# A fused two-layer MLP: the opening loads re-ordered over two queues, with the first transposes gathered ahead of the first matmuls

## The chip, the cores and the metric

The kernel runs on one core of one Trainium2 chip. The metric is the device time of one execution in microseconds (us). The kernel before has a median of 291.05 us in 8 runs (290.72 to 291.46).

## What is computed

```python
B, S, D, F = 1, 2048, 576, 4608          # all tensors bf16
h = einsum("bsd,df->bsf", x, w1) + b1
r = where(h > 0, h, 0)
h = r * r                                 # squared relu
out = einsum("bsf,fd->bsd", h, w2) + b2
```

## The kernel before, in words

The 2048 rows of x are worked on in four blocks of 512 (`SB`). For each block, phase A computes the hidden layer transposed, 36 tiles of 128 hidden features by 512 rows, and phases T and B multiply it with w2. Phase T (`phase_t`) makes the last 128 output columns, phase B (`phase_b`) the other 448. Blocks 0 and 1 go through phase A, then through T and B; then blocks 2 and 3 do the same.

The inner dimension of the first product is 576, four and a half times 128. The first four of the 36 hidden tiles (`a_full`) are computed with four matmuls over 128 inner rows each, and the odd 64 rows with two matmuls that sit side by side in the upper and the lower half of the array (`pair`, L203 and L205). The other 32 hidden tiles (`a_rows`, L188 and L190) split all of the inner dimension into nine pieces of 64 rows, again two matmuls side by side. Because of these halves the transposed x, `xTw`, holds several of its 128-row windows twice, shifted by 64 partitions; the second copies are made by `dup_windows` (L119, L120).

ScalarE takes each hidden tile out of PSUM with bias and relu (L176), VectorE squares it (L177).

The transposed x of blocks 1 to 3 comes from DMA transposes (L126, L127). Block 0 is different, since TensorE would have to wait for these. Its four tiles of 128 rows (`x_sb`) are loaded plainly, transposed on TensorE against an identity (L149) into PSUM banks `tb`, and copied to `xTw` by VectorE (L156, L159) and ScalarE (L158). In the branch `k_outer` of `a_full` the matmuls of the first four hidden tiles are cut into pieces of 256 rows of x (`part(h, k)`, L227, 4 matmuls each) and written out by hand between the transposes: ten transposes (x tiles 0 and 1), part (0,0), five transposes (x tile 2), parts (0,1) and (0,2), five transposes (x tile 3), the parts (0,3) and (1,0), the transpose of the bias rows (`make_b1T`, L166), the rest of the parts, and the two pairs. Until x arrives, TensorE runs seven matmuls on constants (`WARM`, L61 to L63) whose result is not used.

Loads, in their order on each queue:
- SyncE's queue (SP): x tile 0, w1n chunk 0, w1n chunk 1, x tile 3, w1n chunks 2 and 3 (w1n is w1 for the first four hidden tiles, one chunk for each 128 inner rows), two loads of `w_h` (w1 for the other hidden tiles), two loads of `w1n8` (w1's last 64 rows for the first four hidden tiles, in runs of 256 bytes), and the rest of w_h, with the DMA transposes of block 1 between; then the bias b2, w2 in four chunks (`w_sb`), and block 2.
- ScalarE's queue: x tiles 1 and 2, ahead of its activation-table load and a one-element activation (`warm`, L104).
- GpSimd's queue (POOL): the bias b1 as 36 rows of 256 bytes (L98), and 128 single elements of b2 (L100). GpSimd also makes the identity, zeroes the bias rows and converts b2's elements (L102).

`keep` holds the order as written on each engine. `tc.tile_pool` deals out the buffers: PSUM's eight banks are two pools of four, `ps_h` (tag ph) and `ps_o` (tag po).

Of the kernel before, what the change touches and what calls it, by code (L numbers as in the profile page):

```python
# [17 lines left out]
def kernel(  # L18
# [40 lines left out]
    wps = ps_o.tile([P, 512], FP32, name="wps", tag="po")  # L59
    ones = nc.const_aps.tensor(1.0, [P, 512], BF16)  # L60
    WARM = [512] * 6 + [128]  # L61
# [5 lines left out]
    w1n8 = wpool.tile([P, G // 2, P], BF16, name="w1n8")  # L67
# [6 lines left out]
    def load_w1n(eng, k):  # L74
        keep(eng.dma_start(out=w1n[:, k, :], in_=w1[k * P:(k + 1) * P, 0:GW]))  # L75

    def load_w1n8(eng, h):
        src = w1[NK * P:D, 0:GW].rearrange("p (i h f) -> p i h f", h=2, f=P)
        keep(eng.dma_start(out=w1n8[h * H:(h + 1) * H, :, :], in_=src[:, :, h, :]))
# [4 lines left out]

    load_x(nc.sync, 0)
    load_x(nc.scalar, 1)
    load_w1n(nc.sync, 0)
    load_x(nc.scalar, 2)
    load_w1n(nc.sync, 1)
    load_x(nc.sync, 3)  # L90
    for k in range(2, NK):
        load_w1n(nc.sync, k)
# [3 lines left out]
    b1_rows = const.tile([P, P], BF16, name="b1_rows")  # L96
    nc.gpsimd.memset(b1_rows[:], 0.0)
    nc.gpsimd.dma_start(out=b1_rows[0:NFT, :], in_=b1.rearrange("(ft p) -> ft p", p=P))  # L98
    b2_col = const.tile([P, 1], BF16, name="b2_col")
    nc.gpsimd.dma_start(out=b2_col[:], in_=b2[DM:D].rearrange("(d o) -> d o", o=1))  # L100
    b2T = const.tile([P, 1], FP32, name="b2T")
    nc.gpsimd.tensor_copy(out=b2T[:], in_=b2_col[:])  # L102
    warm = const.tile([P, 1], FP32, name="warm")
    keep(nc.scalar.activation(out=warm[:], in_=nc.const_aps.tensor(0.0, [P, 1], FP32), func=ACT.Relu))  # L104

# [25 lines left out]
    W2CH = 9  # L131
# [9 lines left out]
    tb_po = [ps_o.tile([P, 2, HS], BF16, name="tb", tag="po") for _ in range(2)]  # L141
    tb_ph = [ps_h.tile([P, 2, HS], BF16, name="tb", tag="ph") for _ in range(4)]
    half_banks = [tb_ph, None]

    def x_transpose(j, k):
        h, q = divmod(j, 2)
        qc = slice(q * P, (q + 1) * P)
        bank, slot, c0 = (half_banks[h][k], 0, k * P) if k < NK else (half_banks[h][2], 1, D - P)
        keep(nc.tensor.transpose(bank[:, slot, qc], xs[:, j, c0:c0 + P], ident[:]))  # L149

    def x_copies(h):
        hc = slice(h * HS, (h + 1) * HS)
        for k in range(NK):
            src = half_banks[h][k][:, 0, :]
            if k % 2 == 0:
                keep(nc.vector.tensor_copy(out=xT0[:, O + k, hc], in_=src))  # L156
            else:
                keep(nc.scalar.copy(out=xT0[:, O + k, hc], in_=src))  # L158
        keep(nc.vector.tensor_copy(out=xT0[:, E3, hc], in_=half_banks[h][2][:, 1, :]))  # L159


    b1T = const.tile([P, NFT], FP32, name="b1T")

    def make_b1T():
        b1T_ps = ps_o.tile([P, P], BF16, name="b1T_ps", tag="po")
        keep(nc.tensor.transpose(b1T_ps[:], b1_rows[:], ident[:]))  # L166
        keep(nc.vector.tensor_copy(out=b1T[:], in_=b1T_ps[:, 0:NFT]))
# [27 lines left out]
    def a_full(sb, order):  # L195
        xT = xT_blk[sb]
        banks = []
        for g in range(G):
            pool, tag = (ps_o, "po") if g < 2 else (ps_h, "ph")
            banks.append(pool.tile([P, SB], FP32, name="pn", tag=tag))  # L200

        def pair(i, start, stop):
            keep(nc.tensor.matmul(banks[2 * i][:], lhsT=w1n8[0:H, i, :], rhs=xT[0:H, SPC, :],  # L203
                             start=start, stop=stop, skip_group_check=order == "k_outer"))
            keep(nc.tensor.matmul(banks[2 * i + 1][:], lhsT=w1n8[H:P, i, :], rhs=xT[H:P, E3, :],  # L205
                             start=start, stop=stop, skip_group_check=order == "k_outer"))
# [12 lines left out]
        else:  # L219
            if order == "k_outer":  # L220
                tb_new = [ps_h.tile([P, 2, HS], BF16, name="tb", tag="ph") for _ in range(2)]
                half_banks[1] = tb_new + tb_po

# [7 lines left out]
                for j in range(2):  # L231
                    for k in range(NK):
                        x_transpose(j, k)
                for j in range(2):
                    x_transpose(j, NK)
                x_copies(0)
                part(0, 0)
                for k in range(NK + 1):
                    x_transpose(2, k)
                part(0, 1)  # L240
                part(0, 2)
                for k in range(NK + 1):
                    x_transpose(3, k)
                x_copies(1)
                dup_windows(0)
                part(0, 3)
                part(1, 0)
                make_b1T()
                for k in range(1, NK):
                    part(1, k)  # L250
            else:
# [42 lines left out]
    for (j0, j1) in [(0, 1), (1, 2), (2, 4), (4, 6), (6, 8), (8, 10), (10, 12)]:  # L294
        load_w1(nc.sync, 0, j0, j1)
        load_w1(nc.sync, 1, j0, j1)
        if j0 == 0:
            load_w1n8(nc.sync, 0)
            load_w1n8(nc.sync, 1)
    load_xT(1)  # L300
    for (j0, j1) in [(12, 14), (14, 16)]:
        load_w1(nc.sync, 0, j0, j1)
        load_w1(nc.sync, 1, j0, j1)
    keep(nc.sync.dma_start(out=b2_bc[:], in_=b2.partition_broadcast(P)))
    for c in (0, 2, 1, 3):
# [54 lines left out]
```

## Time and profile before

| | us |
|---|---|
| median of 8 runs | 291.05 |
| lowest and highest | 290.72, 291.46 |
| the profiled execution itself | 290.99 |
| its span, first to last instruction | 289.2 |
| TensorE busy in the span | 284.8 (98%) |
| ScalarE busy | 96.6 (33%) |
| VectorE busy | 78.5 (27%) |
| GpSimd busy | 2.2 (1%) |

All durations come from that one profiled execution. A timeline row gives the start, the time from its first start to its last end, the engine, the line, what is written and read, and how often; consecutive equal instructions are merged. The end of a matmul is modelled and overlaps the next one, so the pace of a run of matmuls is read from start to start. In the timeline "SPq" and "ACTq" are the two engines' DMA issues; the transfer itself comes later.

### The profile page before, as it was taken

What the parts mean: (1) busy time and instruction counts of PE and PEld (TensorE: products, weight loads), DVE (VectorE), ACT (ScalarE), POOL (GpSimd) and SP (SyncE); (2) the same over time, 40 slices, a digit from 0 to 9 for tenths busy, and PEclk for the clock granted to TensorE, in tenths of its full rate; (3) what the DMA queues carried; (4) which work ended last, traced back from release to release, by engine and by line L of the source; (5) the groups of instructions that cost most, each with busy time, mean ns of one, the idle gap of its engine ahead of it and who ended that gap; (6) DMA issues with size and microseconds to landing.
All of it is one profiled execution on the core that took longest, in us unless ns stands there. A gap on an engine that the chain in (4) does not pass through costs nothing.

```text
span 289.2 us, 4693 instructions
## 1 busy us (share of the span) xinstructions
PE 284.8 (98%) x2027; PEld 138.8 (48%) x2032; DVE 78.5 (27%) x176; ACT 96.6 (33%) x154; POOL 2.2 (1%) x10
## 2 busy tenths in 40 slices
PE   8999999999999999999999999999999999999996
PEld 4544444444444555555544444444444455555555
DVE  1644544444500200000025444444440001100001
ACT  3666666666500000000027666666670000000000
POOL 3000000000000000000000000000000000000000
PEclk9999999999999999999999999999999999999999
DMA  6999999700001100000000000000000110000000
GB/s 192 219 232 173 261 387 271 121 0 2 0 18 28 44 16 18 16 16 18 16 16 2 1 2 0 2 0 2 0 2 0 36 39 16 16 16 20 32 16 18
DMA packets 31605, 16.52 MB, mean 57 GB/s; under 512 B 15700, under 2 KB 31584, under 8 KB 31584
## 3 DMA queue, kind: packets, MB, share of 16 engines
q1 hardware_dynamic: 31232, 15.91, 22.7%
q8 instruction: 16, 0.26, 0.4%
q10 hardware_dynamic: 288, 0.30, 0.3%
q14 instruction: 5, 0.04, 0.0%
q0 software_dynamic: 64, 0.01, 0.0%
HBM read 11.36 MB, written 2.36 MB: 47 GB/s over the span
## 4 chain that ended last, share of the span: by engine, by line
PE 97%; DMA 1%; SPq 1%; issue 0%; DVE 0%
PE po L289 38%; PE ph L188 24%; PE ph L190 19%; PE pt L270 11%; PE pn L209 4%; DMA w1n<-in_w_dram 1%; PE pn L227 1%; PE pn L203 1%; SPq L75 0%; SPq L72 0%; PE pn L205 0%; DVE o_sb L291 0%; PE tb L149 0%; PE b1T_ps L166 0%
## 5 line engine op out<-in xcount | busy, mean ns | idle before, releaser
L190 PE MATMUL ph<-xTw,w_h 64*128 64x512 bf16 x576 | 124.8, 376 | 0.0
L188 PE MATMUL ph<-xTw,w_h 64*128 64x512 bf16 x576 | 124.7, 376 | 0.0
L289 PE MATMUL po<-w_sb,hT 128*128 128x448 bf16 (+2 forms) x612 | 109.4, 341 | 0.0
L176 ACT ACTIVATE r<-ph,b1T 128x512 bf16<-128x512 f32 x128 | 81.0, 684 | 41.8 <-PE ph L190 22.7
L289 PEld LDWEIGHTS <-hT 128*128 128x128 bf16 x612 | 58.5, 98 | 51.0
L177 DVE TENSOR_TENSOR hT<-r 128x512 bf16<-128x512 bf16 x144 | 61.2, 425 | 76.2 <-ACT r L176 75.6
L188 PEld LDWEIGHTS <-w_h 64*128 64x128 bf16 x576 | 54.1, 94 | 38.5
L190 PEld LDWEIGHTS <-w_h 64*128 64x128 bf16 x576 | 54.1, 94 | 30.0 <-DMA w_h<-in_w_dram 0.4
L291 DVE TENSOR_TENSOR o_sb<-po,b_bc 128x448 bf16<-128x448 f32 (+2 forms) x17 | 10.2, 597 | 125.8 <-PE po L289 125.8
L270 PE MATMUL pt<-hT,w_sb 128*128 128x512 bf16 x142 | 31.3, 379 | 0.1
L176 ACT ACTIVATE r<-pn,b1T 128x512 bf16<-128x512 f32 x16 | 10.3, 687 | 61.2 <-PE pn L205 59.6
L270 PEld LDWEIGHTS <-w_sb 128*128 128x128 bf16 x144 | 14.1, 98 | 17.0
L273 ACT ACTIVATE oT<-pt,b2T 128x512 bf16<-128x512 f32 x4 | 2.7, 687 | 28.3 <-PE pt L270 28.3
L209 PE MATMUL pn<-xTw,w1n 128*128 128x512 bf16 x45 | 10.4, 379 | 0.4 <-issue 0.3
L209 PEld LDWEIGHTS <-w1n 128*128 128x128 bf16 x48 | 4.5, 98 | 6.0 <-issue 0.8
L227 PE MATMUL pn<-xTw,w1n 128*128 128x256 bf16 x32 | 4.2, 273 | 0.5 <-DMA w1n<-in_w_dram 0.4
L63 PE MATMUL wps<-const-bfloat16-1.0 128*128 128x512 bf16 (+1 forms) x7 | 2.8, 579 | 0.8 <-PEq L344 0.8
L227 PEld LDWEIGHTS <-w1n 128*128 128x128 bf16 x32 | 2.9, 98 | 1.1 <-DMA w1n<-in_w_dram 0.6
L119 DVE COPY xTw<-xTw 64x2048 bf16<-64x2048 bf16 x4 | 2.8, 690 | 0.2
L120 DVE COPY xTw<-xTw 64x2048 bf16<-64x2048 bf16 x4 | 2.8, 688 | 0.1
L156 DVE COPY xTw<-tb 128x256 bf16<-128x256 bf16 x4 | 1.1, 291 | 6.0 <-PE tb L149 6.0
L203 PE MATMUL pn<-xTw,w1n 64*128 64x512 bf16 x8 | 2.4, 379 | 0.0
(23 smaller groups left out, 13.7 us busy)
## 6 DMA issues: line engine op xcount, KB each, us to landing
w_sb<-in_w_dram SPq DMA_DIRECT2D x4, 1296.0 KB, 12.7
w_h<-in_w_dram SPq DMA_DIRECT2D x14, 288.0 KB, 6.2
out_dram<-o_sb SPq DMA_DIRECT2D x15, 112.0 KB, 1.7
w_h<-in_w_dram SPq DMA_DIRECT2D x4, 144.0 KB, 3.6
w1n<-in_w_dram SPq DMA_DIRECT2D x4, 128.0 KB, 3.2
out_dram<-ot SPq DMA_DIRECT2D x4, 128.0 KB, 2.0
x_sb<-in_x_dram ACTq DMA_DIRECT2D x2, 144.0 KB, 3.1
x_sb<-in_x_dram SPq DMA_DIRECT2D x2, 144.0 KB, 3.2
```

Of the source, the lines that this page charges most:

```text
L63: keep(nc.tensor.matmul(wps[:, 0:n], lhsT=ones[:, 0:P], rhs=ones[:, 0:n], start=True, stop=True))
L119: keep(nc.vector.tensor_copy(out=xT[0:H, SPC:SPC + 4, :], in_=xT[H:P, E3:E3 + 4, :]))
L176: keep(nc.scalar.activation(out=r[:], in_=bank[:], func=ACT.Relu, bias=b1T[:, ft:ft + 1], scale=1.0))
L177: keep(nc.vector.tensor_tensor(out=hTs[sb][:, ft, :], in0=r[:], in1=r[:], op=ALU.mult))
L188: keep(nc.tensor.matmul(bx[:], lhsT=w1_h[0:H, LO_C[i], jc], rhs=xT[0:H, LO_W[i], :], start=(i == 0), stop=(i == NC - 1)))
L190: keep(nc.tensor.matmul(by[:], lhsT=w1_h[H:P, UP_C[i], jc], rhs=xT[H:P, UP_W[i], :], start=(i == 0), stop=(i == NC - 1)))
L203: keep(nc.tensor.matmul(banks[2 * i][:], lhsT=w1n8[0:H, i, :], rhs=xT[0:H, SPC, :], start=start, stop=stop, skip_group_check=order == "k_o ...
L209: keep(nc.tensor.matmul(banks[g][:], lhsT=w1n[:, k, g * P:(g + 1) * P], rhs=xT[:, O + k, :], start=start, stop=stop))
L227: keep(nc.tensor.matmul(banks[g][:, hc], lhsT=w1n[:, k, g * P:(g + 1) * P], rhs=xT[:, O + k, hc], start=(h == 0 and k == 0), stop=False, s ...
L270: keep(nc.tensor.matmul(pt[:], lhsT=w2_sb[:, ft, DM:D], rhs=hT[:, ft, :], start=(i == 0), stop=(i == NFT - 1)))
L289: keep(nc.tensor.matmul(po[:, 0:d1 - d0], lhsT=hT[:, ft, jj * P:(jj + 1) * P], rhs=w2_sb[:, ft, d0:d1], start=(i == 0), stop=(i == NFT - 1)))
L291: keep(nc.vector.tensor_tensor(out=o_sb[:, d0:d1], in0=po[:, 0:d1 - d0], in1=b2_bc[:, d0:d1], op=ALU.add))
```

## The change

- **x on SP.** All four x tiles go first on SyncE's queue, in order.
- **w1n and b1 on ScalarE's queue.** It issues b1 (its rows zeroed by VectorE now, not GpSimd) and then the four w1n chunks, all of it ahead of the activation-table load.
- **GpSimd loads nothing.** The 128 elements of b2 are loaded on SyncE's queue, behind the last of w_h; GpSimd still converts them.
- **w1n8** is loaded ahead of w_h, as 64 rows of 1024 bytes, twice (all four tiles' columns in both halves of the partitions). w2 comes in two chunks, not four.
- **Transposes.** All 16 full transposes of the four x tiles stand ahead of part (0,0). The odd 64 columns of x are gathered by GpSimd into `xs8`, two x tiles side by side, and cost two transposes in place of four (`transpose_tails`), behind part (0,1).
- **Copies.** Two of eight PSUM copies are ScalarE's, in place of four of eight. The window copies of block 0 are one on ScalarE (1536 elements), and on VectorE four small ones out of PSUM, one of 2048 and one of 512 elements, in place of the two of 2048 elements.
- **Banks.** All transposes use `ps_h`, and the four accumulators of `a_full(0)` use `ps_o`.
- **Warm-up.** Five matmuls of 512 columns and one of 256, in place of six of 512 and one of 128.

```diff
-    wps = ps_o.tile([P, 512], FP32, name="wps", tag="po")
+    wps = ps_h.tile([P, 512], FP32, name="wps", tag="ph")
-    WARM = [512] * 6 + [128]
+    WARM = [512] * 5 + [256]
...
-    w1n8 = wpool.tile([P, G // 2, P], BF16, name="w1n8")
+    w1n8 = wpool.tile([P, GW], BF16, name="w1n8")
...
-        src = w1[NK * P:D, 0:GW].rearrange("p (i h f) -> p i h f", h=2, f=P)
-        keep(eng.dma_start(out=w1n8[h * H:(h + 1) * H, :, :], in_=src[:, :, h, :]))
+        keep(eng.dma_start(out=w1n8[h * H:(h + 1) * H, :], in_=w1[NK * P:D, 0:GW]))
...
+    b1_rows = const.tile([P, P], BF16, name="b1_rows")
+    nc.vector.memset(b1_rows[:], 0.0)
     load_x(nc.sync, 0)
-    load_x(nc.scalar, 1)
-    load_w1n(nc.sync, 0)
-    load_x(nc.scalar, 2)
-    load_w1n(nc.sync, 1)
-    load_x(nc.sync, 3)
-    for k in range(2, NK):
-        load_w1n(nc.sync, k)
+    keep(nc.scalar.dma_start(out=b1_rows[0:NFT, :], in_=b1.rearrange("(ft p) -> ft p", p=P)))
+    for rt in range(1, RT):
+        load_x(nc.sync, rt)
+        load_w1n(nc.scalar, rt - 1, rt)
+    load_w1n(nc.scalar, NK - 1, NK)
...
-    b1_rows = const.tile([P, P], BF16, name="b1_rows")
-    nc.gpsimd.memset(b1_rows[:], 0.0)
-    nc.gpsimd.dma_start(out=b1_rows[0:NFT, :], in_=b1.rearrange("(ft p) -> ft p", p=P))
-    b2_col = const.tile([P, 1], BF16, name="b2_col")
-    nc.gpsimd.dma_start(out=b2_col[:], in_=b2[DM:D].rearrange("(d o) -> d o", o=1))
-    b2T = const.tile([P, 1], FP32, name="b2T")
-    nc.gpsimd.tensor_copy(out=b2T[:], in_=b2_col[:])
...
+    for h in range(2):
+        load_w1n8(nc.sync, h)
+    xs8 = const.tile([P, RT, H], BF16, name="xs8")
+    for h in range(2):
+        keep(nc.gpsimd.tensor_copy(out=xs8[:, 2 * h:2 * h + 2, :], in_=xs[:, 2 * h:2 * h + 2, NK * P:D]))
...
-    W2CH = 9
+    W2CH = 18
...
+    tb = [[ps_h.tile([P, 4, HS], BF16, name="tb", tag="ph") for _ in range(2)] for _ in range(2)]
+
+    def x_transpose(j):
         h, q = divmod(j, 2)
         hc = slice(h * HS, (h + 1) * HS)
+        for bank in range(2):
+            for k in range(2 * bank, 2 * bank + 2):
+                keep(nc.tensor.transpose(tb[h][bank][:, k % 2, q * P:(q + 1) * P], xs[:, j, k * P:(k + 1) * P], ident[:]))
+            for k in range(2 * bank, 2 * bank + 2) if q == 1 else ():
+                copy = nc.scalar.copy if h == 1 and bank == 1 else nc.vector.tensor_copy
+                keep(copy(out=xT0[:, O + k, hc], in_=tb[h][bank][:, k % 2, :]))
...
+    def dup_windows_first():
+        keep(nc.scalar.copy(out=xT0[0:H, E:E + 3, :], in_=xT0[H:P, O:O + 3, :]))
+
+    def transpose_tails():
+        tl = ps_h.tile([P, 2, P], BF16, name="tl", tag="ph")
+        for h in range(2):
+            keep(nc.tensor.transpose(tl[:, h, :], xs8[:, 2 * h:2 * h + 2, :], ident[:]))
+        x8 = xT0.rearrange("p c (h q t) -> p c h q t", h=2, q=2)
+        for q in range(2):
+            keep(nc.vector.tensor_copy(out=x8[H:P, E3, :, q, :], in_=tl[q * H:(q + 1) * H, 0:2, :]))
+        for q in range(2):
+            keep(nc.vector.tensor_copy(out=x8[0:H, SPC, :, q, :], in_=tl[q * H:(q + 1) * H, 0:2, :]))
+        keep(nc.vector.tensor_copy(out=xT0[H:P, SPC:SPC + 4, :], in_=xT0[0:H, O:O + 4, :]))
+        keep(nc.vector.tensor_copy(out=xT0[0:H, E3, :], in_=xT0[H:P, O + 3, :]))
...
-            pool, tag = (ps_o, "po") if g < 2 else (ps_h, "ph")
+            pool, tag = (ps_o, "po") if g < 2 or order == "k_outer" else (ps_h, "ph")
...
-                for j in range(2):
-                    for k in range(NK):
-                        x_transpose(j, k)
-                for j in range(2):
-                    x_transpose(j, NK)
-                x_copies(0)
+                for j in range(RT):
+                    x_transpose(j)
+                dup_windows_first()
                 part(0, 0)
-                for k in range(NK + 1):
-                    x_transpose(2, k)
                 part(0, 1)
+                transpose_tails()
                 part(0, 2)
-                for k in range(NK + 1):
-                    x_transpose(3, k)
-                x_copies(1)
-                dup_windows(0)
                 part(0, 3)
-                part(1, 0)
-                make_b1T()
-                for k in range(1, NK):
+                for k in range(NK):
                     part(1, k)
+                    if k == 1:
+                        make_b1T()
...
-        if j0 == 0:
-            load_w1n8(nc.sync, 0)
-            load_w1n8(nc.sync, 1)
...
+    b2_col = const.tile([P, 1], BF16, name="b2_col")
+    keep(nc.sync.dma_start(out=b2_col[:], in_=b2[DM:D].rearrange("(d o) -> d o", o=1)))
+    b2T = const.tile([P, 1], FP32, name="b2T")
+    keep(nc.gpsimd.tensor_copy(out=b2T[:], in_=b2_col[:]))
     keep(nc.sync.dma_start(out=b2_bc[:], in_=b2.partition_broadcast(P)))
-    for c in (0, 2, 1, 3):
+    for c in range(2):
         load_w2(c)
```

## The prediction

> **What bounds the kernel now.** I read four views in this order. First the page and its chain of work that ended last: TensorE is busy all along.
>
> ```profile
> PE 284.8 (98%) x2027; PEld 138.8 (48%) x2032; DVE 78.5 (27%) x176; ACT 96.6 (33%) x154; POOL 2.2 (1%) x10
> PE   8999999999999999999999999999999999999996
> PE 97%; DMA 1%; SPq 1%; issue 0%; DVE 0%
> ```
>
> The only slice below nine tenths, other than the last, is the first, which is where the change lies. So the whole question is when TensorE starts a_rows(0), its first matmul at L188; what follows is the same work in the same order, at TensorE's pace. Second, TensorE's timeline of the opening.
>
> ```profile
> 0.78 2.82 PE L63 MATMUL wps<-const-bfloat16-1.0 128*128 128x512 bf16 x7 [0.78 <-PEq L344]
> 3.61 0.73 PE L149 MATMUL tb<-ident,x_sb 128*128 128x128 bf16 x10
> 4.44 0.60 PE L227 MATMUL pn<-xTw,w1n 128*128 128x256 bf16 x4
> 4.87 0.45 PE L149 MATMUL tb<-ident,x_sb 128*128 128x128 bf16 x5
> 5.16 0.60 PE L227 MATMUL pn<-xTw,w1n 128*128 128x256 bf16 x4
> 6.11 0.61 PE L227 MATMUL pn<-xTw,w1n 128*128 128x256 bf16 x4 [0.35 <-DMA w1n<-in_w_dram]
> ...
> 7.76 1.47 PE L227 MATMUL pn<-xTw,w1n 128*128 128x256 bf16 x12
> 9.17 0.39 PE L203 MATMUL pn<-xTw,w1n 64*128 64x512 bf16 x1
> ...
> 9.40 0.38 PE L203 MATMUL pn<-xTw,w1n 64*128 64x512 bf16 x1
> ...
> 9.61 0.38 PE L188 MATMUL ph<-xTw,w_h 64*128 64x512 bf16 x1
> ```
>
> x tile 0 releases TensorE at 3.61, a_rows(0) begins at 9.61: 6.00 us. Paces, start to start: a transpose (0.73-0.22)/9 = 0.057 us, a 256-column matmul (1.47-0.27)/11 = 0.109, a pair 0.22. The work is 20 transposes (1.13), 32 part matmuls (3.49), the bias transpose (0.06), two pairs (0.44): 5.12. The other 0.88 is idle: about 0.27 before 4.44 (the first PSUM copy), 0.52 before 6.11 (w1n chunk 2, which lands at 6.06), 0.10 before 9.17 (full to half array).
>
> Third, the transfers: the tile view of x_sb, and the stretches of the opening (the last two columns are the DMA share and GB/s).
>
> ```profile
> DMA to landing us min/median/max: 2.8/3.1/3.6
> ```
> ```profile
> 1.75:2.50 0.75, 0.75 (x4) 0.21 (x2) 0.00 (x0) 0.75 (x1) 0.75 (x2) 1.00 0.74 114
> 2.50:4.25 1.75, 1.74 (x14) 0.84 (x13) 0.15 (x1) 0.75 (x3) 0.17 (x1) 1.00 1.05 368
> 4.25:5.00 0.75, 0.65 (x9) 0.52 (x8) 0.61 (x3) 0.55 (x2) 0.00 (x0) 1.00 0.98 223
> ```
>
> x tile 3, issued at 2.13, is the 3.6: it lands at 5.73. The rate drops from 368 to 223 GB/s where the GpSimd queue's small packets run (3.7 to 5.2 us). Fourth, a_rows(0) has one late weight:
>
> ```profile
> 17.38 0.38 PE L188 MATMUL ph<-xTw,w_h 64*128 64x512 bf16 x1
> 17.67 0.39 PE L190 MATMUL ph<-xTw,w_h 64*128 64x512 bf16 x1
> ```
>
> 0.29 where the pace is 0.22: 0.07 us lost to a w_h load that lands at 17.62.
>
> **What the Trainium skill says.** "DMA: Bandwidth & Descriptors", Issuing engines are not separate DMA queues: queues of different engines share the same DMA engines, and a second queue saves issue time only. The trace agrees: two queues together move 368 GB/s in the opening, SP alone moves up to 392 later. "TensorE: Matmul & The Clock Gate", What's actually happening: the array runs at half clock until it was busy through a window of about 3.4 us, and the windows run freely. The trace agrees: warm-up matmuls start 0.43 apart, twice the later 0.216, and its clock record has full clock from 3.57 for 286.72 us, which is 84 windows of 3.413. "VectorE: DVE Perf Modes", the TRN2 errata: a ScalarE copy between SBUF tiles costs (224 + elements)/1.2 ns; no row here shows one.
>
> **The change, part by part.**
>
> *TensorE.* All 16 full transposes now stand ahead of part (0,0), so it waits for x tile 3. Call its landing T3. Behind it remain: wake-up 0.05 (6.06 to 6.11 above), tile 3's transposes 4 x 0.057 = 0.23, parts 3.49, two tail transposes 0.11, bias 0.06, array change 0.10, pairs 0.44: 4.48. The stalls of 0.27 and 0.52 go, and two transposes (0.11). Break-even with 9.61 is T3 = 5.13, which is 0.60 earlier than now.
>
> *T3.* SP issues four x tiles at its pace of today (0.73, 1.20, 1.66, 2.13), so tile 3 is issued no earlier than now; only what lies ahead of it changes. ScalarE's issues of 0.41 to 0.47 bring b1 and w1n 0 to 2 (402 KB) from about 0.95, behind VectorE's memset. At 2.50 some 86 KB (114 GB/s x 0.75) of the 590 KB of x have moved; from there both queues take half of 368. After 402/184 = 2.18 us, at 4.68, ScalarE's three chunks are through, and the last 102 KB take 0.28 at full rate: 4.96. From last packet to landing it was 0.36 (5.37 to 5.73): T3 = 5.32, take 5.30. This assumes that the dip to 223 goes with the GpSimd loads; if it stays, (368-223) x 0.75 = 109 KB, or 0.30 more. Bounds: 4.8 (issue 2.13 plus the shortest landing in the trace, 2.7) to 5.8 (dip stays, and w1n chunk 3 shares the rate). So a_rows(0) starts at 5.30 + 4.48 = 9.78: **+0.17** (from -0.33 to +0.67).
>
> *New waits.* Transfers of the two hardware queues use eight semaphores in turn, and an issue waits for the landing eight places ahead: today w_h's first issue waits for x tile 1 until 3.74. In the new order w1n 3 waits for x tile 0 (about 3.5), and behind it on ScalarE stand table load (1.28), warm (0.20) and copies: ready near 5.5, needed near 5.8, nothing lost. w1n 3 lands near 5.8, needed by part (0,3) near 7. b1's wait for the memset (0.20 for this size on GpSimd) has w1n behind it; that is in the 0.95. On SP, w1n8 waits for tile 0 and b1 (3.5), then 1; w_h follows near 4.5, 0.8 later than now, and lands near 8.5, needed at 9.8. w_h's wide loads then start near 7.35, where they start at 7.87, because w1n8's issues (2 x 0.65) are no longer between: the load that lands at 17.62 comes some 0.5 earlier and the stall at 17.4 goes: **-0.07**.
>
> *VectorE, ScalarE, GpSimd.* After T3 VectorE has two PSUM copies (0.57), then from tail transposes at T3+1.4 four small ones (4 x 0.29, half the partitions of a row at 0.29), 0.69 (L120's row), 0.25 for 512 elements (between 0.20 and 0.69), bias 0.20: done at T3+3.8; the pairs come at T3+4.0 and need only the small ones, T3+2.6. ScalarE: two copies (0.75) to T3+1.2, then 1536 elements, an estimate from the skill's price of (224+1536)/1.2 = 1.47: T3+2.7, its readers at T3+5.3. GpSimd's gathers are 128 x 128, bounded by the affine select of that size (0.28) and 1.0; cover to T3+1.1. All at nothing, but the cover is thin on VectorE: every us more there than 0.2 to 1.4 would go straight to the path.
>
> *Elsewhere.* b2's column on SP delays b2, w2 and the x transposes by an issue (0.4 to 0.9); w2 has its last issue at 36.3, lands within 13.6, and is first read at 76.1. Nobody waits behind GpSimd's conversion until 84.1. The w2 chunks are as many bytes. PSUM slots: each reuse is of a bank that was emptied over 1 us before. All nothing.
>
> Sum: 290.99 + 0.17 - 0.07 = 291.09; the median lies 0.06 above the profiled execution: **291.15**.
>
> **The rivals.** The measurement can tell about 0.2%, 0.58 us, from no change; 290.47 and 291.63 are the limits.
>
> *x comes sooner (0.13).* Without the dip and with tile 0 alone at the front, T3 could be 4.8: 9.28, so -0.33 - 0.07: 290.65. For it: SP's packets are x alone. Against: half the rate goes to w1n. It passes 290.47 only with T3 below 4.6, about half of this case.
>
> *The clock rises late (0.16), the other side.* The warm-up ends near 0.78 + 0.38 + 4 x 0.43 + 0.21 = 3.09, where it ended at 3.6, and until T3 TensorE has 12 transposes only. In the window 0.15 to 3.57 it was busy 2.79 of 3.41 us, 82%; now 2.3 to 2.4, 69%. It decides if 69% doesn't open the gate: the next window ends at 6.98, and half pace from 5.3 to there costs 1.68/2 = 0.84: 292.0. Still another window: 2.5, 293.6. Up to T3 a late gate is free.
>
> *Local copies bind (0.06).* VectorE's chain or GpSimd's gather is over 1.4 late against T3+4.0: about +0.7, 291.9.
>
> *The dip stays (0.05).* T3 = 5.8: +0.50, 291.6.
>
> **How the numbers follow.** The forecast case has 0.60. Faster by over 0.2%: half of the first rival, 0.07. Slower: 0.15 of the clock, 0.05 of the copies, 0.01 of the dip: 0.21. Within: 0.72. Range: 290.5 (T3 4.7 and the runs' spread) to 292.0 (clock one window late), leaving about 0.17 out.
>
> **What would show it.** Right: x tile 3 lands near 5.3, part (0,0) starts by 5.6, no gap among the 32 parts, L188 starts at 9.8, no 0.29 step near 17.5, no rate dip at 4.25 to 5. Wrong: T3 below 4.8 or above 5.6; transposes or parts at 0.11 or 0.21 pace behind T3 (clock); an idle gap before the tails or L203 (copies); any stall after 12 us that is new.

## The result, and the profile after

The changed kernel is slower: a median of 293.4 us (291.76 to 294.66, 11 runs) beside 291.01 for the kernel before (290.58 to 291.61, 31 runs). The ratio, which is one of means, is 1.0075, 95% interval 1.0062 to 1.0089, or 1.8 to 2.6 us. The spread grew too, from 1.0 to 2.9 us. The profiled execution took 293.40 us, its span is 291.5; that of before took 290.99. So the two profiles differ by 2.41 us, as the medians do (2.39), and the working below uses the profiles.

The page of the kernel after, busy time, the row of slices, and the chain that ended last:

```profile
PE 285.6 (98%) x2024; PEld 139.8 (48%) x2029; DVE 79.3 (27%) x181; ACT 97.4 (33%) x153; POOL 1.5 (1%) x9
PE   6999999999999999999999999999999999999996
PE 97%; DMA 2%; SPq 0%; issue 0%; DVE 0%
```

TensorE still sets the end and is as full as before in all slices but the first, which fell from 8 tenths to 6, and the chain now has 2% of DMA. The loss is in the opening. TensorE's timeline of it (the transposes are L146 now, the parts L228, the tails L159, the pairs L207 and L209, a_rows L192 and L194):

```profile
0.77 2.51 PE L63 MATMUL wps<-const-bfloat16-1.0 128*128 128x512 bf16 x6 [0.77 <-PEq L338]
3.07 1.06 PE L146 MATMUL tb<-ident,x_sb 128*128 128x128 bf16 x8
5.67 0.61 PE L146 MATMUL tb<-ident,x_sb 128*128 128x128 bf16 x4 [1.54 <-DMA x_sb<-in_x_dram]
6.78 0.61 PE L146 MATMUL tb<-ident,x_sb 128*128 128x128 bf16 x4 [0.51 <-DMA x_sb<-in_x_dram]
7.18 1.91 PE L228 MATMUL pn<-xTw,w1n 128*128 128x256 bf16 x8
8.89 0.36 PE L159 MATMUL tl<-ident,xs 128*128 128x128 bf16 x2
9.08 1.91 PE L228 MATMUL pn<-xTw,w1n 128*128 128x256 bf16 x16
...
10.88 1.04 PE L228 MATMUL pn<-xTw,w1n 128*128 128x256 bf16 x8
11.85 0.39 PE L207 MATMUL pn<-xTw,w1n 64*128 64x512 bf16 x1
...
12.29 0.38 PE L192 MATMUL ph<-xTw,w_h 64*128 64x512 bf16 x1
```

Two things are to be seen. TensorE waits 1.54 us for x tile 2 and 0.51 for x tile 3. And behind tile 3 it runs at half pace: the first eight of the parts' matmuls take 1.91 us, as long as the sixteen that begin at 9.08. The trace's clock record has full clock from 9.04; before it was 3.57. Below, the moment from which the record shows full clock is called the opening of the clock gate. a_rows(0) begins at 12.29, where it began at 9.61: 2.68 later. The tile view of x_sb in the kernel after, and then its opening in two stretches, up to 2.50 and on to 6.37, which is 0.36 before x tile 3 lands (last column GB/s):

```profile
DMA to landing us min/median/max: 2.2/3.1/4.6
```
```profile
0.00:2.50 2.50, 1.73 (x5) 0.65 (x6) 0.11 (x1) 0.00 (x0) 0.70 (x6) 1.00 0.26 70
2.50:6.37 3.87, 2.23 (x15) 1.30 (x13) 0.88 (x4) 1.49 (x2) 0.29 (x1) 1.00 0.90 263
```

Tile 3, issued at 2.12, is the 4.6: it lands at 6.73 (before 5.73). The stretch moved 263 GB/s. PEclk is 1.00 in both: the column doesn't show the half pace, the matmuls' starts and the clock record do.

Later on, time comes back. The place of the late w_h load, now at 20 us, shows no step, and at the switch from a_rows(1) to the next `a_full`, at 72 us in the kernel before and 74 us in the kernel after, the two half-array streams stand differently. First before, then after:

```profile
71.85 0.38 PE L190 MATMUL ph<-xTw,w_h 64*128 64x512 bf16 x1
71.85 0.38 PE L203 MATMUL pn<-xTw,w1n 64*128 64x512 bf16 x1
72.07 0.38 PE L205 MATMUL pn<-xTw,w1n 64*128 64x512 bf16 x1
72.07 0.38 PE L203 MATMUL pn<-xTw,w1n 64*128 64x512 bf16 x1
72.28 0.38 PE L205 MATMUL pn<-xTw,w1n 64*128 64x512 bf16 x1
```
```profile
74.24 0.38 PE L192 MATMUL ph<-xTw,w_h 64*128 64x512 bf16 x1
74.24 0.38 PE L194 MATMUL ph<-xTw,w_h 64*128 64x512 bf16 x1
74.45 0.38 PE L207 MATMUL pn<-xTw,w1n 64*128 64x512 bf16 x1
74.46 0.38 PE L209 MATMUL pn<-xTw,w1n 64*128 64x512 bf16 x1
```

Before, the lower half's last L190 runs beside the upper half's L203, and a lone L205 is left at 72.28 with nothing beside it. The stall at 17.4 had put the halves one matmul out of step, and they stayed so. After, they are in step and the slot of 0.21 us is not spent. With the 0.08 of the stall itself that is -0.29. Experiment 4 shows that this need not be the change's doing. The sum: +2.68 - 0.29 = +2.39, and the last matmul moved from 286.27 to 288.66, by +2.39.

### The profile page after: what moved, and what is told of

Read it like the earlier page. It is cut to its first block, busy times and chain, and to the rows that moved or that the text cites. A ratio compares the mean times of both kernels' runs of the same rounds, so it can differ in the third digit from the quotient of the medians.

```text
span 291.5 us, 4693 instructions
## 1 busy us (share of the span) xinstructions
PE 285.6 (98%) x2024; PEld 139.8 (48%) x2029; DVE 79.3 (27%) x181; ACT 97.4 (33%) x153; POOL 1.5 (1%) x9
## 4 chain that ended last, share of the span: by engine, by line
PE 97%; DMA 2%; SPq 0%; issue 0%; DVE 0%
PE ph L192 42%; PE po L282 37%; PE pt L263 11%; PE pn L213 3%; DMA x_sb<-in_x_dram 2%; PE pn L228 1%; PE ph L194 1%; PE pn L207 1%; SPq L72 0%; PE tb L146 0%; DVE o_sb L284 0%; PE tl L159 0%; PE b1T_ps L170 0%; PE pn L209 0%
## 5 line engine op out<-in xcount | busy, mean ns | idle before, releaser
L192 PE MATMUL ph<-xTw,w_h 64*128 64x512 bf16 x576 | 124.6, 376 | 0.0
L194 PE MATMUL ph<-xTw,w_h 64*128 64x512 bf16 x576 | 124.6, 376 | 0.0
L192 PEld LDWEIGHTS <-w_h 64*128 64x128 bf16 x576 | 54.1, 94 | 68.3
L194 PEld LDWEIGHTS <-w_h 64*128 64x128 bf16 x576 | 54.1, 94 | 0.0
L213 PEld LDWEIGHTS <-w1n 128*128 128x128 bf16 x48 | 4.5, 98 | 6.0 <-issue 0.8
L228 PE MATMUL pn<-xTw,w1n 128*128 128x256 bf16 x32 | 4.7, 310 | 0.0
L146 PE MATMUL tb<-ident,x_sb 128*128 128x128 bf16 x16 | 2.3, 309 | 2.0 <-DMA x_sb<-in_x_dram 2.0
L228 PEld LDWEIGHTS <-w1n 128*128 128x128 bf16 x32 | 3.5, 112 | 0.6
L146 PEld LDWEIGHTS <-x_sb 128*128 128x128 bf16 x16 | 1.6, 134 | 3.0 <-DMA x_sb<-in_x_dram 3.0
L149 DVE COPY xTw<-tb 128x256 bf16<-128x256 bf16 x6 | 1.4, 283 | 5.4 <-PE tb L146 5.4
```

The source lines that it names most:

```text
L146: keep(nc.tensor.transpose(tb[h][bank][:, k % 2, q * P:(q + 1) * P], xs[:, j, k * P:(k + 1) * P], ident[:]))
L192: keep(nc.tensor.matmul(bx[:], lhsT=w1_h[0:H, LO_C[i], jc], rhs=xT[0:H, LO_W[i], :], start=(i == 0), stop=(i == NC - 1)))
L194: keep(nc.tensor.matmul(by[:], lhsT=w1_h[H:P, UP_C[i], jc], rhs=xT[H:P, UP_W[i], :], start=(i == 0), stop=(i == NC - 1)))
L213: keep(nc.tensor.matmul(banks[g][:], lhsT=w1n[:, k, g * P:(g + 1) * P], rhs=xT[:, O + k, :], start=start, stop=stop))
L228: keep(nc.tensor.matmul(banks[g][:, hc], lhsT=w1n[:, k, g * P:(g + 1) * P], rhs=xT[:, O + k, hc], start=(h == 0 and k == 0), stop=False, s ...
```

## The experiments

The theory after the result: at full clock a_rows(0) begins 4.48 us after x tile 3 lands, as forecast; what went wrong is that tile 3 lands at 6.7, not 5.3, and that the clock gate opens late, because TensorE idles while it waits. Rivals: the shorter warm-up or the new compute order costs the time by itself; b1 ahead of w1n on ScalarE's queue delays the loads; GpSimd's loads are what held x back before.

One profiled execution of each kernel, in us (the median of the timed runs stands with each experiment; ratios are against the kernel before, timed beside it, with their 95% intervals). A load counts up in sixteen parts as they land, and TensorE waits for the last of them; "middle" is the ninth:

| kernel | x tile 3 lands: middle, last of its 16 parts | full clock from | a_rows(0) starts | profiled time |
|---|---|---|---|---|
| before | 5.44, 5.73 | 3.57 | 9.61 | 290.99 |
| after | 5.88, 6.73 | 9.04 | 12.29 | 293.40 |
| 1 after, long warm-up | 5.33, 6.29 | 4.71 | 10.77 | 291.88 |
| 2 after, old load order | 4.95, 5.27 | 10.03 | 12.03 | 293.13 |
| 3 before, new loads | 5.70, 6.48 | 9.48 | 12.08 | 293.40 |
| 4 before, short warm-up | 5.13, 5.71 | 5.20 | 9.55 | 290.73 |
| 5 long warm-up, b1 last | 5.73, 6.53 | 5.68 | 11.00 | 292.17 |
| 6 x on two queues, then w1n | 4.10, 4.37 | 4.34 | 10.38 | 291.78 |
| 7 old load order, long warm-up | 5.13, 5.32 | 3.45 | 9.80 | 291.15 |
| 8 before, no GpSimd loads | 4.98, 6.13 | 6.19 | 10.08 | 291.36 |
| 9 before, wider first w_h load | 5.29, 6.08 | 4.83 | 10.71 | 292.11 |
| 10 the same, w1n 2 ahead of x tile 3 | 5.58, 6.25 | 3.90 | 9.93 | 291.28 |
| 11 w1n behind the table load | 4.79, 5.36 | (no record) | 11.42 | 292.43 |
| 12 after, waits filled | 5.84, 6.29 | 3.85 | 10.77 | 292.70 |
| 13 x, then w1n, all on SP | 4.44, 4.95 | 3.41 | 10.44 | 291.68 |
| 14 before, w1n 2 and w1n8 ahead | 5.37, 5.54 | 5.87 | 9.79 | 290.98 |

**1. The changed kernel with a warm-up that lasts until the third x tile.**

```diff
-    WARM = [512] * 5 + [256]
+    WARM = [512] * 12
```

> The changed kernel with 12 warm-up matmuls of 512 columns instead of five and one of 256; nothing else. Clock theory: TensorE no longer idles between the warm-up and x tile 3, full clock comes by about 6 us, the 32 part matmuls run at 0.109 us and a_rows(0) starts 4.4 us after x tile 3 lands, about 11.2 if that is again at 6.73: 1.1 us off the 293.4, some 292.2, and the runs lie closer together. Rival (the clock only looks late, the delay is the late x tile and the new copies): time stays near 293.4.

Measured: 292.22 us (291.88 to 292.44, 5 runs), ratio 1.0033 [1.0021, 1.0045]. TensorE's timeline of it:

```profile
5.29 0.83 PE L146 MATMUL tb<-ident,x_sb 128*128 128x128 bf16 x12
6.33 0.40 PE L146 MATMUL tb<-ident,x_sb 128*128 128x128 bf16 x4 [0.21 <-DMA x_sb<-in_x_dram]
6.57 1.04 PE L228 MATMUL pn<-xTw,w1n 128*128 128x256 bf16 x8
```

The same eight matmuls take 1.04 instead of 1.91. With twelve matmuls that compute nothing, in place of six, the median is 1.2 us lower, and the spread falls from 2.9 us (11 runs) to 0.6 (5 runs). Tile 3 landed at 6.29: 6.29 + 4.48 = 10.77, and a_rows(0) starts at 10.77. So 12.29 - 10.77 = 1.52 is 0.44 of landing and 1.08 of clock. What is left against before is the landing.

**2. The changed kernel with the old load order** (the w1n8 form, b2's place and all compute as after; b1 behind tile 2 on ScalarE's queue).

```diff
     load_x(nc.sync, 0)
+    load_x(nc.scalar, 1)
+    load_w1n(nc.sync, 0, 1)
+    load_x(nc.scalar, 2)
+    load_w1n(nc.sync, 1, 2)
+    load_x(nc.sync, 3)
+    for k in range(2, NK):
+        load_w1n(nc.sync, k, k + 1)
     keep(nc.scalar.dma_start(out=b1_rows[0:NFT, :], in_=b1.rearrange("(ft p) -> ft p", p=P)))
-    for rt in range(1, RT):
-        load_x(nc.sync, rt)
-        load_w1n(nc.scalar, rt - 1, rt)
-    load_w1n(nc.scalar, NK - 1, NK)
```

> The changed kernel with x tiles and w1n chunks in the order and on the queues of the kernel before (x0, w1n0, w1n1, x3, w1n2, w1n3 on SyncE, x1 and x2 on ScalarE), b1 behind x2 on ScalarE's queue. Load-order theory: x tile 3 lands near 5.7 as in the kernel before, not at 6.73, and a_rows(0) starts near 10.2 plus what the clock costs: 291.3 at full pace, up to 292.5 with a late clock. Rival (TensorE's order alone costs, whatever the loads): near 293.4.

Measured: 291.64 us (290.85 to 293.19, 13 runs), ratio 1.0024 [1.0009, 1.0039]. The runs fall into two groups, eight at 290.85 to 291.78 and five at 292.54 to 293.19. The profiled one is of the upper group; its timeline (transposes L149, parts L231):

```profile
5.32 0.61 PE L149 MATMUL tb<-ident,x_sb 128*128 128x128 bf16 x4 [0.28 <-DMA x_sb<-in_x_dram]
5.72 1.91 PE L231 MATMUL pn<-xTw,w1n 128*128 128x256 bf16 x8
...
7.64 3.08 PE L231 MATMUL pn<-xTw,w1n 128*128 128x256 bf16 x16
```

Tile 3 lands at 5.27, as the prediction had it for the changed kernel, and still a_rows(0) starts at 12.03: with 4.48 it would be 9.75, so the late gate alone cost 2.28 in this execution. Both theories' parts are real, and the clock is an effect of its own.

**3. The kernel before with the new loads** (both queues, w1n8 ahead of w_h, nothing on GpSimd; transposes, copies, banks and warm-up as before).

```diff
     load_x(nc.sync, 0)
-    load_x(nc.scalar, 1)
-    load_w1n(nc.sync, 0)
-    load_x(nc.scalar, 2)
...
+    keep(nc.scalar.dma_start(out=b1_rows[0:NFT, :], in_=b1.rearrange("(ft p) -> ft p", p=P)))
+    for rt in range(1, RT):
+        load_x(nc.sync, rt)
+        load_w1n(nc.scalar, rt - 1)
+    load_w1n(nc.scalar, NK - 1)
```

> The kernel before with the loads of the changed kernel (x on SyncE, b1 and w1n on ScalarE, w1n8 ahead of w_h, b2 column late on SyncE, GpSimd loading nothing); TensorE's order, the copies and the warm-up stay. Load-order theory: w1n chunk 1 lands near 6.5 and holds parts (0,1) on, a_rows(0) near 10.9, so some 292.0. Transposes-first theory (the loads are harmless, only waiting for all four x tiles costs): a_rows(0) at 9.6 or earlier and 290.7 to 291.0.

Measured: 291.56 us (291.11 to 293.65, 22 runs), ratio 1.0029 [1.0015, 1.0043]; sixteen runs at 291.11 to 291.98, six at 293.06 to 293.65. Tile 3 lands at 6.48. The loads alone make the kernel slower, even under the old compute order, though the median by some 0.5 us and not 2.4. The profiled run is one of the upper group and loses as much as the changed kernel: it has full clock from 9.48, and TensorE waits for w1n ahead of part (0,0):

```profile
5.52 1.03 PE L223 MATMUL pn<-xTw,w1n 128*128 128x256 bf16 x4 [0.85 <-DMA w1n<-in_w_dram]
6.88 1.91 PE L223 MATMUL pn<-xTw,w1n 128*128 128x256 bf16 x8
```

Why the sixteen other runs lose less isn't shown, since none of them has a profile; the old order does parts (0,0) to (0,2) while tile 3 is under way, which may be the reason.

**4. The kernel before with the short warm-up.** It tests whether the shorter warm-up is itself the cost.

```diff
-    WARM = [512] * 6 + [128]
+    WARM = [512] * 5 + [256]
```

> The kernel before with the short warm-up of the changed kernel (five of 512 and one of 256). Clock theory in its idle form (what counts is the waiting until x tile 3, not the length of the warm-up): 291.0 to 291.3. Clock theory in its warm-up form (the warm-up has become too short to open the gate): 291.8 or more, with a wide spread.

Measured: 291.22 us (290.55 to 291.53, 13 runs), ratio 0.9999 [0.9991, 1.0007]: no difference. The gate opened at 5.20, with the first two blocks of transposes and part (0,0) at half pace, and a_rows(0) began at 9.55. In the old order a somewhat late gate is paid for out of waits that follow anyway. The shorter warm-up is not a cost by itself; what decides is what TensorE does after it.

This profile shows one thing more. All loads are issued as before, but the w_h load that landed at 17.62 in before lands at 15.87 here. There is no stall at 17.4, and the two half-array streams are in step at the switch:

```profile
71.71 0.38 PE L203 MATMUL pn<-xTw,w1n 64*128 64x512 bf16 x1
71.72 0.38 PE L205 MATMUL pn<-xTw,w1n 64*128 64x512 bf16 x1
```

From a_rows(0) to the last matmul it takes 276.37 us, as in after; before it was 276.66. So the -0.29 between the profiles of before and after is a difference that executions of the old load order show among themselves. That the change brought it about is not shown.

**5. Experiment 1 with b1 behind w1n** on ScalarE's queue.

```diff
-    WARM = [512] * 5 + [256]
+    WARM = [512] * 12
...
-    keep(nc.scalar.dma_start(out=b1_rows[0:NFT, :], in_=b1.rearrange("(ft p) -> ft p", p=P)))
...
     load_w1n(nc.scalar, NK - 1, NK)
+    keep(nc.scalar.dma_start(out=b1_rows[0:NFT, :], in_=b1.rearrange("(ft p) -> ft p", p=P)))
```

> The changed kernel with the long warm-up of 12 matmuls and b1 behind the four w1n chunks on ScalarE's queue, not ahead of them; to be set against the same kernel with b1 ahead (292.22 us, x tile 3 landing at 6.29). If the bias load is what slows the transfers after 2.7 us: the long first packets of w1n chunk 0 (0.6 to 1.2 us) go, x tile 3 lands near 5.5 and the time is near 291.4. If it is w1n itself, read on the second queue beside x: x tile 3 stays near 6.3 and the time near 292.2.

Measured: 292.17 us (292.13 to 292.26, 4 runs), ratio 1.0042 [1.0027, 1.0057], as experiment 1. The stretch 2.50 to 4.25 moves 302 GB/s where experiment 1 has 228 and after 189, so b1's place does change the early rate. But tile 3 lands at 6.53, no sooner. The rival on b1 falls.

**6. x on both queues, w1n behind it.**

```diff
-    WARM = [512] * 5 + [256]
+    WARM = [512] * 8
...
+    for rt in range(0, RT, 2):
+        load_x(nc.sync, rt)
+        load_x(nc.scalar, rt + 1)
+    for k in range(0, NK, 2):
+        load_w1n(nc.sync, k, k + 1)
+        load_w1n(nc.scalar, k + 1, k + 2)
```

> The changed kernel with eight warm-up matmuls, x tiles 0 and 2 on SyncE and 1 and 3 on ScalarE, then the w1n chunks in turn on both, b1 last. If what delays x tile 3 is w1n's share of the rate and its slow packets: x tile 3 lands near 4.4, part (0,0) starts near 5 when w1n chunk 0 is there, a_rows(0) near 9.3, some 290.5. If the opening is limited in bytes whatever the order: the wait moves from x tile 3 to w1n (chunks at 5 to 6.5) and the time is 291.0 to 291.5.

Measured: 291.49 us (291.09 to 291.78, 11 runs), ratio 1.0015 [1.0006, 1.0024]. All of x lands by 4.37 (tiles 1 and 3 are ScalarE's), 2.4 us sooner than after. The wait moves: w1n lands at 5.83 to 7.03, part (0,0) begins only at 5.88, and a_rows(0) begins at 10.38. x first is bought with w1n last.

**7. Experiment 2 with a long warm-up.** If the clock made the two groups, the upper one must vanish.

```diff
+    WARM = [512] * 11
```

> The changed kernel with the old order of x and w1n (x tile 3 landed at 5.27 there) and 11 warm-up matmuls. Clock theory: the slower group of that kernel's runs (292.5 to 293.2) disappears and all lie with the faster group, 290.9 to 291.6, median about 291.2; a_rows(0) near 9.8. Rival: two groups remain, so they come from something else than the idle array.

Measured: 291.62 us (291.07 to 292.11, 17 runs), ratio 1.0019 [1.0011, 1.0027]. No run is in the upper group. Tile 3 lands at 5.32, 5.32 + 4.48 = 9.80, and a_rows(0) begins at 9.80. Its opening, up to 2.50 and on to 0.36 before tile 3 lands:

```profile
0.00:2.50 2.50, 1.73 (x5) 0.65 (x6) 0.11 (x1) 0.16 (x1) 0.70 (x6) 1.00 0.23 49
2.50:4.96 2.46, 2.46 (x18) 1.27 (x16) 0.00 (x0) 1.32 (x2) 0.29 (x1) 1.00 1.04 336
```

Here 49 x 2.50 + 336 x 2.46 = 950 KB had moved 0.36 us before tile 3 landed, at 336 GB/s. By the same mark after had moved 70 x 2.50 + 263 x 3.87 = 1193 KB, at 263. x, w1n and b1 together are 590 + 524 + 9 = 1123 KB: in the changed order tile 3 is through only when nearly all of w1n is through too (507 of its 524 KB by the packets, and 79 KB of w1n8). The landing and the start of a_rows(0) are what the prediction gave the changed kernel (5.30 and 9.78), with another load order; and the kernel is no faster than before.

**8. The kernel before without GpSimd's loads** (b1 on ScalarE's queue behind tile 2, b2's column late on SP).

```diff
+    nc.vector.memset(b1_rows[:], 0.0)
+    keep(nc.scalar.dma_start(out=b1_rows[0:NFT, :], in_=b1.rearrange("(ft p) -> ft p", p=P)))
...
-    nc.gpsimd.dma_start(out=b1_rows[0:NFT, :], in_=b1.rearrange("(ft p) -> ft p", p=P))
-    nc.gpsimd.dma_start(out=b2_col[:], in_=b2[DM:D].rearrange("(d o) -> d o", o=1))
```

> The kernel before with b1 on ScalarE's queue behind x tile 2 and b2's column late on SyncE, nothing else. If GpSimd's small packets cause the rate dip at 4.25 to 5: x tile 3 lands near 5.3 instead of 5.73, w1n chunk 2 near 5.65 instead of 6.06, TensorE's 0.52 wait shrinks to about 0.1, a_rows(0) at 9.2: 290.6. If not: 291.0 to 291.2.

Measured: 291.19 us (290.94 to 291.38, 12 runs), ratio 1.0007 [0.9999, 1.0016]. The stretches in it:

```profile
2.50:4.25 1.75, 1.67 (x10) 0.81 (x9) 0.00 (x0) 1.30 (x2) 0.00 (x0) 1.00 1.12 359
4.25:5.00 0.75, 0.75 (x9) 0.68 (x7) 0.33 (x2) 0.47 (x2) 0.00 (x0) 1.00 0.92 292
```

The dip is half gone, 292 where before has 223. The middle part of tile 3 lands at 4.98, where it is 5.44 in before and 5.13 in experiment 4, which both have GpSimd's loads. So these may hold x back by some tenths, as the prediction took it. But the last part lands at 6.13: one packet of w1n chunk 1, ahead of it on SP, took 1.16 us from 4.00 on. With the same x and w1n order experiments 2 and 7 have the last part at 5.27 and 5.32. What a tile's landing is worth is decided by its slowest part, and the time shows nothing gained (in this profile the gate is late too, at 6.19).

**12. The changed kernel with its waits filled.** 20 transposes of tile 1 and 8 of tile 2 are repeated into the bank; this extra TensorE work is overwritten by the real transposes. The warm-up stays short.

```diff
+        for _ in range((0, 20, 8, 0)[j]):
+            keep(nc.tensor.transpose(tb[h][0][:, 0, q * P:(q + 1) * P], xs[:, j, 0:P], ident[:]))
```

> The changed kernel, short warm-up and all, with 20 repeated transposes of x tile 1 and 8 of x tile 2 (into the same PSUM places, ahead of the real ones) that fill the waits for the next tile. Clock theory in its idle form: every window of 3.41 us from 0.8 on is busy by over 77%, full clock by 4.2 to 7, the time as with the long warm-up, 292.0 to 292.5, in one group. If the warm-up's length is what counts: 293.4 and a wide spread.

Measured: 292.49 us (five runs at 291.93 to 292.70, one at 293.96), ratio 1.0053 [1.0034, 1.0073]. In the profile the gate opens at 3.85, tile 3 lands at 6.29 and a_rows(0) begins at 10.77, to the hundredth as in experiment 1, with the warm-up of after. So it is the idle wait, not the warm-up, that holds the gate shut. The median is not as good as experiment 1's: the profiled run has a w_h wait of 0.66 at 14.65, which experiment 1 has not; what makes that load late stays open, and so does what the run at 293.96 met.

**11. x alone on SP, w1n behind the activation-table load** in ScalarE's program, to hold w1n back without giving it SP.

```diff
+    WARM = [512] * 8
...
+    keep(nc.scalar.activation(out=warm[:], in_=nc.const_aps.tensor(0.0, [P, 1], FP32), func=ACT.Relu))
+    for k in range(NK):
+        load_w1n(nc.scalar, k, k + 1)
```

> The changed kernel with eight warm-up matmuls, x tiles alone on SyncE and the w1n chunks behind the activation-table load on ScalarE's queue (issued from about 2.9 on, not 1.6). If x tile 3 is late because w1n shares the rate: it lands at 4.6 to 5.0, the wait moves to w1n chunk 0 (about 5.8), a_rows(0) at 10.0 to 10.4, some 291.4. If the slow stretch at 2.5 to 4.25 comes whatever the second queue does: x tile 3 at 5.5 or later and 292 or more.

Measured: 292.43 us (292.25 to 292.82, 4 runs), ratio 1.0049 [1.0035, 1.0063]. Chunk 0 was issued at 1.66, while the table load of 1.60 to 2.88 ran, the others at 2.92 to 5.09. Tile 3 lands at 5.36, between the two forecasts, with some 160 KB of w1n and w1n8 alongside, and TensorE then waits 0.69 and 0.26 for w1n. Its matmuls run at half pace up to 6.58. This experiment decides little by itself.

**13. x and then w1n, all on SP;** b1 alone on ScalarE's queue.

```diff
+    WARM = [512] * 8
...
+    for rt in range(RT):
         load_x(nc.sync, rt)
+    keep(nc.scalar.dma_start(out=b1_rows[0:NFT, :], in_=b1.rearrange("(ft p) -> ft p", p=P)))
+    for k in range(NK):
+        load_w1n(nc.sync, k, k + 1)
```

> The changed kernel with eight warm-up matmuls and the four w1n chunks behind the x tiles on SyncE; b1 stays first on ScalarE's queue, which issues nothing else in the opening. If the share of w1n on the second queue makes x tile 3 late: it lands at 4.6 to 5.0, w1n chunk 0 near 5.3 and chunk 3 near 6.5, a_rows(0) at 9.6 to 9.9, some 291.1. If the slow stretch from 2.5 to 4.25 goes with b1 on ScalarE's queue: the rate there stays near 200 GB/s, x tile 3 lands at 5.5 or later, 291.8 or more.

Measured: 291.47 us (291.38 to 292.19, 20 runs), ratio 1.0021 [1.0013, 1.0028]. The tile view of x_sb, and TensorE's timeline (parts L227):

```profile
DMA to landing us min/median/max: 2.2/2.5/2.9
```
```profile
5.39 0.61 PE L227 MATMUL pn<-xTw,w1n 128*128 128x256 bf16 x4
6.67 0.61 PE L227 MATMUL pn<-xTw,w1n 128*128 128x256 bf16 x4 [0.66 <-DMA w1n<-in_w_dram]
```

The longest flight of an x tile is 2.9, where it is 4.6 in the changed kernel with the same x issues at the same times: tile 3 lands at 4.95. What is different ahead of it is that w1n isn't on the second queue. So w1n's share of the transfers is what makes x late. Between the two kernels it is a matter of bytes and not of the rate: 0.36 before the landing 686 KB had moved by the packets, in place of 1193, at 255 GB/s from 2.50 on, no faster than in the changed kernel. The time isn't saved: w1n now comes one chunk at a time behind x, and part (0,1) waits until 6.67.

**9, 10 and 14. Can the kernel before be mended where it waits?** Experiment 9 makes w_h's first load wider, to take the late one at 17.4 away; 10 also puts w1n chunk 2 ahead of x tile 3, for the wait of 0.52; 14 keeps w_h as before, with chunk 2 ahead of x tile 3 and w1n8 ahead of w_h.

```diff
-    for (j0, j1) in [(0, 1), (1, 2), (2, 4), (4, 6), (6, 8), (8, 10), (10, 12)]:
+    for (j0, j1) in [(0, 2), (2, 4), (4, 6), (6, 8), (8, 10), (10, 12)]:
```

> The kernel before with the first two w_h steps (0,1), (1,2) loaded as one step (0,2): two issues fewer, runs of 512 bytes. If the late w_h load at 17.4 costs 0.07 at once and another 0.21 where the two half-array streams end out of step, its removal gives 0.29: 290.75, ratio 0.9990. If it costs only its 0.07: 290.95, not to be told from no change.

Measured: 292.15 us (291.76 to 292.41, 5 runs), ratio 1.0036 [1.0024, 1.0049], a miss. The timeline says why: w1n8 stands behind the wider load on SP, and the first pair waits for it.

```profile
8.76 0.71 PE L227 MATMUL pn<-xTw,w1n 128*128 128x256 bf16 x5
10.23 0.39 PE L203 MATMUL pn<-xTw,w1n 64*128 64x512 bf16 x1 [0.76 <-DMA w1n<-in_w_dram]
```

```diff
+    load_w1n(nc.sync, 2)
     load_x(nc.sync, 3)
-    for k in range(2, NK):
-        load_w1n(nc.sync, k)
+    load_w1n(nc.sync, 3)
...
+    for (j0, j1) in [(0, 2), (2, 4), (4, 6), (6, 8), (8, 10), (10, 12)]:
```

> The same, and w1n chunk 2 ahead of x tile 3 on SyncE. The wait of 0.52 us for w1n chunk 2 (landing 6.06) shrinks to about 0.2, x tile 3 lands near 6.0 and is needed at about 6.1: a_rows(0) at 9.3, together 290.4, ratio 0.998. If x tile 3 then holds TensorE instead: 290.75, as with the w_h edit alone.

Measured: 292.09 us (291.28 to 292.38, 9 runs), ratio 1.0033 [1.0023, 1.0044]. The wait of 0.52 is gone, but the first pair still begins 0.41 late behind w1n8, where 0.10 is usual. The profiled run is the fastest of the nine, so what the others lose is not seen.

```diff
+    load_w1n(nc.sync, 2)
     load_x(nc.sync, 3)
+    load_w1n(nc.sync, 3)
+    load_w1n8(nc.sync, 0)
+    load_w1n8(nc.sync, 1)
...
-        if j0 == 0:
-            load_w1n8(nc.sync, 0)
-            load_w1n8(nc.sync, 1)
```

> The kernel before with two moves on SyncE's queue: w1n chunk 2 ahead of x tile 3, and w1n8 ahead of w_h as in the changed kernel (w_h's steps as they were). The wait for w1n chunk 2 shrinks from 0.52 to about 0.2, and no load of w1n8 or w_h is late: a_rows(0) at 9.3 and no step near 17.4: 290.4 to 290.7. If the w_h loads behind w1n8 now come late, a new gap at or behind L188 and 291 or more.

Measured: 291.01 us (290.83 to 291.29, 13 runs), ratio 0.9999 [0.9991, 1.0008]. Neither the 0.52 nor the stall at 17.4 is there, and the half-array streams are in step at the switch; but in the profiled run the gate opened at 5.87 and a_rows(0) began at 9.79, 0.18 later. 0.18 - 0.29 leaves 290.88, measured 290.98. After experiment 4 the missing stall can't be put down to the edit. None of the fourteen versions beats the kernel before.

## Why the prediction was wrong, by its own steps

The sum was 290.99 + 0.17 - 0.07. Measured it is 290.99 + 2.68 - 0.29 = 293.38, beside 293.40.

**4.48 us from T3 to a_rows(0): right.** Experiments 1, 5 and 7, where the clock is full in time, give 10.77, 11.00 and 9.80 from landings at 6.29, 6.53 and 5.32: 4.48, 4.47 and 4.48. The break-even T3 of 5.13 follows from it and stands.

**T3 = 5.30: wrong by 1.43, the larger failure.** It was 402 KB of ScalarE's and 590 KB of x at 368 GB/s from 2.50: (992 - 86)/368 = 2.46, last packet at 4.96. With the same 0.36 ahead of the landing one comes to 6.37, when (1193 - 175) KB had moved at 263 GB/s. Two terms were off. The bytes: w1n chunk 3 went along, which the prediction had only in its upper bound, and the start of w1n8, which it had not; less the 89 KB more that were there at 2.50, that is (1018 - 906)/368 = 0.30 us. The rate: 1018/263 - 1018/368 = 1.10 us. By the trace x's last packet with data ends at 6.18 and the landing is 0.55 behind it, so some 0.2 of the 1.10 is a longer way from the data to the landing. The 368 was another order's, and the bound of 5.8 let it fall in one stretch of 0.75 us only. It does not carry over: from 2.50 to 0.36 before tile 3's landing it is 326 in before itself, 336 in experiment 7, 297 in experiment 5, 255 in experiment 13.

The packets show where part of the rate is lost. Ten packets of w1n chunk 0 in the kernel after, begun between 2.85 and 3.75, took 0.55 to 1.23 us each, where the middle one of its kind takes 0.046, and what is behind such a packet would have to stand (the trace doesn't say which DMA engine carried it): tile 3's parts land from 4.80 to 6.73, the middle one at 5.88. They sum to 7.9 us; by an estimate the lost 1.10 us of all sixteen DMA engines is 17.6, so less than half of it. In experiment 1 three such packets took 1.06 to 1.25, the middle part landed at 5.33, where the prediction had the whole tile, and the last at 6.29. The prediction reckoned with a mean rate, and a tile is there with its slowest part. Packets over 0.5 us, from 1.2 to 6 us, sum to 7.9, 4.1, 6.2 and 5.5 us in the four kernels with b1 first and all of w1n behind it ahead of the table load (after, 1, 3, 12), to 4.0 in before, and to between none and 3.7 in the others. What makes them long is not settled: b1 last (experiment 5) leaves four of them, but tile 3 comes no sooner; w1n chunk 0 is then issued at 0.73 and not at 1.60, so more of it is alongside.

"The Trainium skill", page "DMA: Bandwidth & Descriptors", section Issuing engines are not separate DMA queues, which the prediction used, says that loads from different queues run on the same DMA engines and interleave. The trace fits this: w1n on a second queue did not let x come by itself, in the changed order both were through nearly together. That the dip goes with GpSimd's loads was about half right (experiment 8) and too small to matter.

**"Up to T3 a late gate is free", and 0.16 for the clock: the mechanism right, its weight wrong.** This rival is part of what happened, on top of the late T3. It was priced with a window of 0.15 to 3.57 as in the profile of before, 69% busy (its 82% for before is the warm-up's whole span; matmul by matmul it is 77); but the windows stood elsewhere, and 69% would not have opened the gate either (experiment 3, last section). With tile 2 at 5.62 the window 2.21 to 5.63 was 50% busy, the gate opened at 9.04, and everything from 6.78 to 9.04 ran at half pace: +1.08 (experiment 1; the medians differ by 1.2, with experiment 1's earlier landing in it). 1.60 of landing and 1.08 of clock make up the 2.68. The prediction also took the two as separate cases, where one can bring the other: waiting for a late tile is idle time, and idle time can keep the gate shut.

**-0.07 for the late w_h load: its sign came true by luck, its size was wrong.** Between the two profiles it is -0.29. The prediction counted the delay at the stall and not that it leaves the two halves of the array out of step up to the switch. And it took the stall for a property of the load order, but experiment 4 has that order and no stall (the load lands at 15.87 in place of 17.62). Nor did w_h follow as forecast: its first issue came at 5.42 and not near 4.5, since w1n chunk 0, eight places ahead, landed at 5.41; a_rows(0) was later still, so nothing waited.

**The local copies: right.** ScalarE's copy of 1536 elements, in the kernel after:

```profile
8.10 1.47 ACT L154 COPY xTw<-xTw 64x1536 bf16<-64x1536 bf16 x1
```

It was forecast at 1.47 from "The Trainium skill", page "VectorE: DVE Perf Modes", the TRN2 errata, and takes 1.47. GpSimd's gathers took 0.29 each, VectorE's four small copies 0.29 to 0.30, its copy of 512 elements 0.29 (forecast 0.25). No matmul waited for any of them.

**"Elsewhere, nothing": right** in this profile: no wait behind 12.3 us is new.

## What to carry to other kernels

If several loads go out in one burst, moving one to the front moves the wait to another: x tile 3 landed between 4.37 and 6.73 in these orders, and no other order started a_rows(0) sooner than the 9.61 of before, which works on each tile as it comes. Gathering all transposes ahead of the first matmul makes the whole opening depend on the last tile and leaves TensorE idle ahead of it, which is paid for in waiting and then, if the gate stays shut, in half clock. A rate read from one order of loads is no price for another one: take the lowest rate that the trace shows as one end, and count all bytes in flight beside the load that is waited for.

## What the runs showed of the hardware that was not expected

- **How busy a window must be.** Taking each matmul from its start for the time of its columns at half pace (0.43 us for 512), windows of 3.413 us (the clock records last 283.306 and 286.72 us, 83 and 84 of these) ahead of the opening were busy 77, 77, 77, 78, 78, 84% or more in the runs whose gate opened, and at most 75, 69, 67, 59, 50% in windows after which it stayed shut (75 in experiment 2, 69 in experiment 3, 50 in after). By this count, in these profiles, the limit lies between 75 and 77%.
- **The windows' phase differs from run to run.** The openings stand between 3.41 and 10.03 us. "The Trainium skill", page "TensorE: Matmul & The Clock Gate", section What's actually happening, says that the windows run freely, and the runs fit this: the same kernel falls into two groups 1.5 to 2 us apart (experiments 2 and 3), by where the windows happen to lie, and a warm-up that fills the wait takes the upper group away (experiment 7). That the groups are the gate's is shown by a profile of the upper group in each of experiments 2 and 3 and by experiment 7; for the runs without a profile no record shows when the gate opened.
- **Single packets 25 times as long as their kind:** 1.16 to 1.25 us beside 0.046, in the opening; experiment 2 had none above 0.5.
- **Two half-array streams keep a shift.** After one late weight of 0.08 us in before one half stays a matmul behind, and the end of the stream costs another 0.21 us. Experiments 7 and 12 show the same: waits of 0.12 and 0.66 us at w_h, 0.34 and 0.88 lost by the last matmul.
- **ScalarE issues a load during its table load:** in experiment 11 an issue at 1.66 lies within the table load from 1.60 to 2.88.
